# Norm matmuls in another PSUM bank, squares in pairs, and square sums carried over three groups, in a fused attention and channel-mix kernel

## The chip, the cores and the metric

The kernel runs on one core of a Trainium2 chip. The metric is the device time of one execution in microseconds (us). Most executions of a kernel agree within 0.3%; those with a mean granted TensorE clock of 0.988 to 0.997 in place of 0.998 to 1.000 are mostly 0.3 to 4 us longer than the fastest, and a few at 0.998 to 1.000 are longer too, by up to 1 us. I give the lowest time beside the median where that matters.

## The reference

Two stages, with B = 4, N = 6208 and 256 channels, all in fp32:

```python
qn = q / (np.linalg.norm(q, axis=1, keepdims=True) + 1e-06)   # norms over the 6208 rows
kn = k / (np.linalg.norm(k, axis=1, keepdims=True) + 1e-06)
s = kn.transpose(0, 2, 1) @ qn / tau                          # 256 x 256 per batch
a = softmax(s);  x = v @ a
xk = mu_k * x + (1 - mu_k) * x_prev;  xr = mu_r * x + (1 - mu_r) * x_prev
kk = np.maximum(xk @ w_k, 0) ** 2                             # 1024 hidden
out = sigmoid(xr @ w_r) * (kk @ w_v)
```

## The kernel before

After a head that treats the covariance of batch 0, a main loop goes through 48 blocks of 512 rows and one of leftovers. A block has eight steps j. Beside each block's channel mix, the loop builds the covariance and the column norms of the next batch from row groups of 512 (12 full ones per batch and one of 64 rows). Matmuls write into tiles in PSUM. A `tag` names a place there, which with one buffer holds one tile at a time: the next tile of that tag waits until the one before has been copied out. The parts that matter, cut:

```python
def up(i, fh):                                     # hidden slice fh of block i
    kT_ps = ps.tile([P, M], F32, name="kT_ps", tag="kT", bufs=3)
    # ... two matmuls of w_k with xk into kT_ps ...
    kr = p2.tile([P, M], BF16, name="kr", tag="kr", bufs=4)
    nc.scalar.activation(kr[:, :m], kT_ps[:, :m], AF.Relu, scale=RH)

def square(i, fh):
    nc.vector.tensor_tensor(st[i, "kk"][:, fh, :m], kr[:, :m], kr[:, :m], op=OP.mult)

# gate_mm: g_ps lies in the single PSUM bank "g"; x_half: xT_ps lies in the single bank "xT"
# unit(b, g, s): covariance matmuls of a quarter group, then ACT squares it into G["sq", s // 2]

def take_sum():                                    # two adds on DVE for each group
    if w == 1:
        nc.vector.tensor_tensor(G["sq", 0], G["sq", 0], G["sq", 1], op=OP.add)      # 128 x 1024 fp32
        return
    if w == 2:
        nc.vector.tensor_tensor(t1, G["sq", 0][:, 0], G["sq", 0][:, 1], op=OP.add)  # to bf16

def take_norm():                                   # one set of four one-column matmuls for each group
    n_ps = ps.tile([P, 4], F32, name="n_ps", tag="g")
    # ... n_ps[:, 2i+h] = t1 slice (as weights) @ ones ...
    nc.scalar.copy(ssq[b][:, :, g], n_ps)

# in the loop, step j of block i (cut):
up(i + 1, j)
if j == 0: square(i, 7)
if j > 0:  square(i + 1, j - 1)
# ... gate_mm in steps 0, 1, 4, 5; down (the second product, reads kk); x_half in steps 0 and 2 ...
# ... mix_delta in step 4, mix(n, "xk", 0) in step 5, mix(n, "xk", 1) in step 6 ...
# softmax pieces; norms in steps 3 and 7; sums in steps 2, 3, 6, 7
```

## Time and profile before

| | before |
|---|---|
| time, median of 3 runs | 517.29 us (517.14 to 517.46) |
| profiled span | 515.3 us |
| TensorE / VectorE / ScalarE busy | 96% / 88% / 85% |
| matmuls for norms in the loop | 156 |

TensorE is PE in the profile (PEld for its weight loads), VectorE DVE, ScalarE ACT, GpSimd POOL. The profile's own busy share hides how little TensorE loses, so the measure used from here on is this: a weight load starts with the matmul ahead of it, so the starts of loads give the pace of the matmuls (medians 216, 109, 56 and 25 ns for 512, 256, 128 and 1 columns). What the gaps have beyond the pace is **stall**. In the text below it is netted: a late load is often followed by a gap that is shorter than the pace, and both are counted.

The next fence is the timeline of before around one of the longest stalls: start in us, length in us, engine, line, what it does, and in brackets how long the engine had been idle and what released it.

```profile
389.06 0.42 DVE L348 TENSOR_TENSOR kk<-kr 128x512 bf16<-128x512 bf16 x1
389.40 0.75 DVE L324 SCALAR_TENSOR_TENSOR xk<-delta,mu_k_t,X 128x512 bf16<-128x512 bf16 x1
390.06 0.76 DVE L348 TENSOR_TENSOR kk<-kr 128x512 bf16<-128x512 bf16 x2
390.20 0.38 PE L339 MATMUL kT_ps<-xk,w_k_sb 128*128 128x512 bf16 x1 [0.60 <-DVE xk L324]
```

The matmul of the next block's first slice waits for the second half of xk, which VectorE starts (389.40) only after a square (389.06). The chain of waits that ended last is of no use here: it holds 2.5 us near the end only.

### The profile page before, as it was taken

How to read it: one execution, taken by the hardware profiler on the slowest of the kernel's cores; microseconds unless marked ns; L12 is line 12 of the kernel's file. 1: busy time of each engine (PE TensorE's matmuls, PEld its weight loads, DVE VectorE, ACT ScalarE, POOL GpSimd, SP SyncE). 2: the span in 40 equal slices, each digit the busy share in tenths (PEclk: the TensorE clock that was granted, in tenths of full speed). 3: DMA queues.
4: the chain of work that ended last, by engine and by line, in shares of the span. 5: the costliest groups of instructions: out<-in, count | busy, mean ns of one | idle time of the engine just before them, and what ended most of it. 6: DMA issues, size and time to landing. Idle time of an engine off the chain costs nothing. (4 is left out here: it accounts for less than half of the span.)

```text
span 515.3 us, 10233 instructions
## 1 busy us (share of the span) xinstructions
PE 492.3 (96%) x3723; PEld 340.5 (66%) x3786; DVE 451.3 (88%) x899; ACT 435.7 (85%) x832; POOL 104.5 (20%) x145
## 2 busy tenths in 40 slices
PE   4699999999999999999999999999999999999996
PEld 2474676767667677677666767667666666666675
DVE  3468899999999999999999999999989888888884
ACT  5778999999989898899999899899787877777773
POOL 0047523332431231221251132100031000000000
PEclk9999999999999999999999999999999999999999
DMA  8999999999999999599699999962298673332113
GB/s 313 396 321 188 181 201 207 194 201 186 186 186 207 164 170 174 115 173 155 109 185 216 167 178 165 142 129 71 62 170 141 122 126 95 94 88 76 58 67 102
DMA packets 143202, 83.51 MB, mean 162 GB/s; under 512 B 51184, under 2 KB 139824, under 8 KB 143152
## 3 DMA queue, kind: packets, MB, share of 16 engines
q0 software_dynamic: 65808, 33.01, 50.1%
q1 hardware_dynamic: 77184, 49.72, 39.5%
q8 instruction: 29, 0.48, 0.4%
q14 instruction: 21, 0.17, 0.1%
q10 hardware_dynamic: 160, 0.13, 0.1%
HBM read 78.71 MB, written 25.43 MB: 202 GB/s over the span
## 5 line engine op out<-in xcount | busy, mean ns | idle before, releaser
L342 ACT ACTIVATE kr<-kT_ps 128x512 bf16<-128x512 f32 (+1 forms) x392 | 232.5, 595 | 37.0 <-PE kT_ps L339 29.8
L387 PE MATMUL v_ps<-w_v_sb,kk 128*128 128x256 bf16 x1536 | 230.4, 273 | 0.5
L339 PE MATMUL kT_ps<-xk,w_k_sb 128*128 128x512 bf16 (+1 forms) x725 | 218.9, 377 | 3.0 <-DVE xk L324 1.3
L348 DVE TENSOR_TENSOR kk<-kr 128x512 bf16<-128x512 bf16 (+1 forms) x392 | 161.7, 417 | 35.1 <-ACT kr L342 31.4
L387 PEld LDWEIGHTS <-kk 128*128 128x128 bf16 x1536 | 150.2, 98 | 57.6
L430 ACT ACTIVATE sq<-qk 128x512 f32<-128x512 bf16 (+1 forms) x147 | 93.2, 634 | 0.0
L339 PEld LDWEIGHTS <-w_k_sb 128*128 128x128 bf16 x784 | 74.8, 98 | 22.0 <-issue 1.0
L358 PE MATMUL g_ps<-w_r_sb,xr 128*128 128x256 bf16 x388 | 73.9, 272 | 2.5 <-ACT ssq L467 1.3
L260 ACT CAST X<-xT_ps 128x512 bf16<-128x512 f32 x94 | 55.5, 590 | 20.0 <-PE xT_ps L258 19.3
L324 DVE SCALAR_TENSOR_TENSOR xr<-delta,mu_r_t,X 128x512 bf16<-128x512 bf16 x96 | 71.5, 745 | 0.0
L358 PEld LDWEIGHTS <-xr 128*128 128x128 bf16 x388 | 37.8, 98 | 49.0 <-issue 5.9
L324 DVE SCALAR_TENSOR_TENSOR xk<-delta,mu_k_t,X 128x512 bf16<-128x512 bf16 x94 | 70.1, 745 | 0.0
L400 DVE SCALAR_TENSOR_TENSOR res<-res,v_ps 128x512 f32<-128x512 f32 x96 | 65.3, 680 | 0.0
L416 POOL DMA_DIRECT2D qk<-in_q_dram x39 | 28.6, 734 | 164.8 <-ACT sq L430 136.7
L393 ACT ACTIVATE res<-g_ps 128x512 f32<-128x512 f32 x97 | 57.8, 596 | 0.4 <-PE g_ps L358 0.4
L258 PE MATMUL xT_ps<-vT,a_sb 128*128 128x512 bf16 x188 | 55.9, 379 | 0.2 <-ACT X L285 0.2
L426 PE MATMUL s_ps<-qk 128*128 128x256 bf16 (+1 forms) x294 | 56.1, 272 | 0.0
L227 POOL DMA_DIRECT2D v_bf<-in_v_dram x48 | 37.3, 781 | 52.4 <-DMA vT<-v_bf 47.4
L448 DVE TENSOR_TENSOR sq<-sq 128x1024 f32<-128x1024 f32 x36 | 43.9, 1219 | 1.0 <-ACT sq L430 1.0
L426 PEld LDWEIGHTS <-qk 128*128 128x128 bf16 (+1 forms) x294 | 26.6, 97 | 12.1 <-issue 1.3
L313 DVE TENSOR_TENSOR delta<-X 128x1024 bf16<-128x1024 bf16 x48 | 32.9, 686 | 0.1
L416 POOL DMA_DIRECT2D qk<-in_k_dram x39 | 28.9, 741 | 6.8 <-DMA qk<-in_q_dram 2.1
(73 smaller groups left out, 235.1 us busy)
## 6 DMA issues: line engine op xcount, KB each, us to landing
out_dram<-res SPq DMA_DIRECT2D x48, 512.0 KB, 3.3
v_bf<-in_v_dram POOLq DMA_DIRECT2D x48, 256.0 KB, 8.1
qk<-in_q_dram POOLq DMA_DIRECT2D x36, 256.0 KB, 8.5
qk<-in_k_dram POOLq DMA_DIRECT2D x36, 256.0 KB, 9.5
f<-in_q_dram SPq DMA_DIRECT2D x12, 512.0 KB, 8.3
f<-in_k_dram SPq DMA_DIRECT2D x11, 512.0 KB, 9.1
vT<-v_bf SPq DMA_TRANSPOSE x44, 6.7
w_k_sb<-in_moe_w_k_dram POOLq DMA_DIRECT2D x1, 512.0 KB, 6.3
```

Of the source, the lines that this page charges most:

```text
L258: nc.tensor.matmul(xT_ps, a_sb[:, b, ih, dh * P:(dh + 1) * P], vT[:, :, ih, :], start=ih == 0, stop=ih == 1)
L324: nc.vector.scalar_tensor_tensor(o[:, dh], st[i, "d"][:, dh], mu[:, dh:dh + 1], X[:, dh, c:c + M], op0=OP.mult, op1=OP.add)
L339: nc.tensor.matmul(kT_ps[:, :m], w_k_sb[:, dh, fh * P:(fh + 1) * P], xk[:, dh, :m], start=dh == 0, stop=dh == 1)
L342: nc.scalar.activation(kr[:, :m], kT_ps[:, :m], AF.Relu, scale=RH)
L348: nc.vector.tensor_tensor(st[i, "kk"][:, fh, :m], kr[:, :m], kr[:, :m], op=OP.mult)
L358: nc.tensor.matmul(g_ps[:, s % 2], xr[:, dh, s * P:(s + 1) * P], w_r_sb[:, dh, :], start=s % 2 == 0 and dh == 0, stop=dh == 1, skip_group_ ...
L387: nc.tensor.matmul(v_ps[:, s % 2], kk[:, fh, s * P:(s + 1) * P], w_v_sb[:, fh, :], start=s % 2 == 0 and fh == 0, stop=fh == 7, skip_group_ ...
L393: nc.scalar.activation(st[i, "res"][:, 2 * u:2 * u + 2], st.pop((i, "g", u)), AF.Tanh, scale=0.5)
L400: nc.vector.scalar_tensor_tensor(r, r, 1.0, st.pop((i, "v", u)), op0=OP.add, op1=OP.mult)
L416: nc.gpsimd.dma_start(qk[:rows, :n, i], src_rows(t, b, g))
L426: nc.tensor.matmul(cov[b][:, ih, :], qk[:rows, s, 1, ih * P:(ih + 1) * P], qk[:rows, s, 0, :], start=g == GORD[0] and s == 0 and ih == 0, ...
L430: nc.scalar.activation(G["sq", s // 2][:rows, s % 2], qk[:rows, s], AF.Square)
```

## The change

Intent: take norm matmuls off TensorE (one set for three groups in batches 2 and 3), pay for the added fp32 adds by squaring two slices in one operation, and take the norms out of the gate's bank. Norms also run at least two steps after their sum. The core of the diff (cut: bookkeeping of columns, and the flag `bank_x`, which is set when another piece takes the place of x in that step; `T` counts steps):

```diff
-        kr = p2.tile([P, M], BF16, name="kr", tag="kr", bufs=4)
-        nc.scalar.activation(kr[:, :m], kT_ps[:, :m], AF.Relu, scale=RH)
+        if fh % 2 == 0:
+            st[i, "kr", fh // 2] = p2.tile([P, 2, M], BF16, name="kr", tag="kr", bufs=3)
+        nc.scalar.activation(st[i, "kr", fh // 2][:, fh % 2, :m], kT_ps[:, :m], AF.Relu, scale=RH)
...
-        nc.vector.tensor_tensor(st[i, "kk"][:, fh, :m], kr[:, :m], kr[:, :m], op=OP.mult)
+        if fh % 2 == 0:
+            return
+        nc.vector.tensor_tensor(st[i, "kk"][:, fh - 1:fh + 1, :m], kr[:, :, :m], kr[:, :, :m], op=OP.mult)
...
+                m = (GORD.index(g) - 1) % MERGE if b > 1 else 0      # MERGE = 3
+                if m == 0:
+                    sums.append((b, g, 1))                           # acc = sq0 + sq1
+                else:
+                    sums.append((b, g, 3))                           # acc += sq0
+                    sums.append((b, g, 4))                           # acc += sq1
+                if b == 1 or m == MERGE - 1:
+                    sums.append((b, g, 2))                           # t1 = the halves of acc added
...
-        norms.append((b, g, t1))
+        norms.append((b, g, t1, T + 2))
-        n_ps = ps.tile([P, 4], F32, name="n_ps", tag="g")
+        n_ps = ps.tile([P, 4], F32, name="n_ps", tag="xT")
-            nc.scalar.copy(hold["bc"], broadcast(hold["dq"], "g"))
+            nc.scalar.copy(hold["bc"], broadcast(hold["dq"], "xT"))
...
-            if j > 0 and 0 <= i + 1 < NBLK:
+            if j > 0 and j != 6 and 0 <= i + 1 < NBLK:
                 square(i + 1, j - 1)
...                                                                  # after mix(n, "xk", 1):
+            if j == 6 and 0 <= i + 1 < NBLK:
+                square(i + 1, j - 1)
...
-            elif j in (3, 7) or j in (2, 6) and len(norms) > 1:
+            if j in (4, 6) and not bank_x or j in (3, 5) and len(norms) > 1:
                 take_norm()
```

More of the change, by code (lines that the diff above doesn't have):

```diff
@@ L340, in up @@
                              start=dh == 0, stop=dh == 1)
-        kr = p2.tile([P, M], BF16, name="kr", tag="kr", bufs=4)
-        nc.scalar.activation(kr[:, :m], kT_ps[:, :m], AF.Relu, scale=RH)
-        st[i, "kr", fh] = kr
+        if fh % 2 == 0:
+            st[i, "kr", fh // 2] = p2.tile([P, 2, M], BF16, name="kr", tag="kr", bufs=3)
+        nc.scalar.activation(st[i, "kr", fh // 2][:, fh % 2, :m], kT_ps[:, :m], AF.Relu, scale=RH)
     def square(i, fh):
         m = size(i)
-        kr = st.pop((i, "kr", fh))
-        nc.vector.tensor_tensor(st[i, "kk"][:, fh, :m], kr[:, :m], kr[:, :m], op=OP.mult)
+        if fh % 2 == 0:
+            return
+        kr = st.pop((i, "kr", fh // 2))
+        nc.vector.tensor_tensor(st[i, "kk"][:, fh - 1:fh + 1, :m], kr[:, :, :m], kr[:, :, :m], op=OP.mult)
     def gate_mm(i, s):
@@ L422, in unit @@
             ssq[b] = pn.tile([P, 4, NB + 1], F32, name="ssq")
+            ncol[b] = 0
         G = groups[b, g]
@@ L432, in unit @@
             if n == S:
-                sums.append((b, g, 1))
-                sums.append((b, g, 2))
+                m = (GORD.index(g) - 1) % MERGE if b > 1 else 0
[6 more added lines that the diff above has]
+                    sums.append((b, g, 2))
             else:
@@ L439 @@
     norms = []
+    acc = {}
+    MERGE = 3
     def take_sum():
@@ L447, in take_sum @@
         if w == 1:
-            nc.vector.tensor_tensor(G["sq", 0], G["sq", 0], G["sq", 1], op=OP.add)
+            acc[b] = pq.tile([P, 2, 2, C], F32, name="acc", tag="acc", bufs=2)
+            nc.vector.tensor_tensor(acc[b], G["sq", 0], G["sq", 1], op=OP.add)
+            return
+        if w > 2:
+            nc.vector.tensor_tensor(acc[b], acc[b], G["sq", w - 3], op=OP.add)
             return
@@ L451, in take_sum @@
         if w == 2:
-            nc.vector.tensor_tensor(t1, G["sq", 0][:, 0], G["sq", 0][:, 1], op=OP.add)
+            nc.vector.tensor_tensor(t1, acc[b][:, 0], acc[b][:, 1], op=OP.add)
         else:
             nc.vector.tensor_copy(t1[:rows], G["sq", 0][:rows, 0])
-        norms.append((b, g, t1))
+        norms.append((b, g, t1, T + 2))
     def take_norm():
-        if not norms:
+        if not norms or norms[0][3] > T:
             return
-        b, g, t1 = norms.pop(0)
+        b, g, t1, _ = norms.pop(0)
         rows, n = rows_of(g)
-        n_ps = ps.tile([P, 4], F32, name="n_ps", tag="g")
+        n_ps = ps.tile([P, 4], F32, name="n_ps", tag="xT")
         for i in range(2):
@@ L466, in take_norm @@
                                  start=i == 0 and h == 0, stop=True, skip_group_check=True)
-        nc.scalar.copy(ssq[b][:, :, g], n_ps)
+        nc.scalar.copy(ssq[b][:, :, ncol[b]], n_ps)
+        ncol[b] += 1
         if g == GORD[-1]:
@@ L471 @@
     ssq = {}
+    ncol = {}
     s_sb = {}
@@ L482, in a @@
         def a():
-            hold["n"] = root(ssq[b], 4)
+            hold["n"] = root(ssq[b][:, :, :ncol[b]], 4)
         def a2():
@@ L634 @@
                 v_load(i + 7)
-            bank_g = False
-            if chain and (chain[0] is None or chain[0].__name__ != "bcast" or j in (3, 7)):
+            bank_x = i >= 0 and i % NB == 6 and j == 4
+            if chain and (chain[0] is None or chain[0].__name__ != "bcast" or j in (4, 6)):
                 f = chain.pop(0)
@@ L639 @@
                     f()
-                    bank_g = f.__name__ == "bcast"
-            if bank_g:
-                pass
-            elif j in (3, 7) or j in (2, 6) and len(norms) > 1:
+                    bank_x = f.__name__ == "bcast"
+            if j in (4, 6) and not bank_x or j in (3, 5) and len(norms) > 1:
                 take_norm()
```

## The prediction

> **What bounds the kernel now.** I read the page first, engine totals and then the 40 slices, and after that the groups by shape, the waits, and the timeline around single waits of TensorE.
>
> ```profile
> span 515.3 us, 10233 instructions
> ...
> PE 492.3 (96%) x3723; PEld 340.5 (66%) x3786; DVE 451.3 (88%) x899; ACT 435.7 (85%) x832; POOL 104.5 (20%) x145
> ...
> PE   4699999999999999999999999999999999999996
> PEld 2474676767667677677666767667666666666675
> DVE  3468899999999999999999999999989888888884
> ACT  5778999999989898899999899899787877777773
> ```
>
> TensorE (PE) is full from the fourth slice on; VectorE (DVE) and ScalarE (ACT) are nearly full, but behind it. Busy time cannot say how full PE is, so I took the start times of all weight loads (a load starts with the matmul ahead of it, and no load is missing from the trace). From one to the next the median is 109 ns for a matmul of 256 columns, 216 ns for 512, and 25 ns for the one-column norm matmuls. What goes beyond those medians is stall: 22.8 us in the whole span, 14.1 of them in the head before 48 us, which the change does not touch. So in the 467 us of the main loop PE stands still for 8.8 us. No change on DVE or ACT alone can win more than that; the rest must come from fewer matmuls.
>
> The waits of PE, and the groups concerned:
>
> ```profile
> PE g_ps L358 <- ACT ssq L467: 1.3, 4, 0.5
> PE kT_ps L339 <- DVE xk L324: 1.3, 3, 0.6
> PE n_ps L465 <- DVE t L452: 0.5, 1, 0.5
> ```
>
> ```profile
> L348 DVE TENSOR_TENSOR kk<-kr 128x512 bf16<-128x512 bf16 x384 | 159.3, 420 | 32.7 <-ACT kr L342 29.1
> ...
> L448 DVE TENSOR_TENSOR sq<-sq 128x1024 f32<-128x1024 f32 x36 | 43.9, 1219 | 1.0 <-ACT sq L430 1.0
> ...
> L313 DVE TENSOR_TENSOR delta<-X 128x1024 bf16<-128x1024 bf16 x48 | 32.9, 686 | 0.1
> ...
> L452 DVE TENSOR_TENSOR t<-sq 128x512 bf16<-128x512 f32 x36 | 24.6, 684 | 0.0
> ...
> L465 PE MATMUL n_ps<-ones_b,t 128*128 128x1 bf16 x144 | 8.7, 164 | 0.6 <-DVE t L452 0.5
> ```
>
> Two stretches of the timeline, start and length in us. In the first, four norm matmuls are over 0.10 us after they began, though their records last 0.24. In the second, the gate matmuls (g_ps) wait until ACT has copied the norms out of the bank that both use; ACT is late because the softmax's two exponentials came first.
>
> ```profile
> 253.72 0.24 PE L465 MATMUL n_ps<-ones_b,t 128*128 128x1 bf16 x4
> 253.82 0.38 PE L426 MATMUL s_ps<-qk 128*128 128x256 bf16 x2
> ```
>
> ```profile
> 269.41 0.50 ACT L202 ACTIVATE e_sb<-t_sb,nrm_o 128x256 f32<-128x256 f32 x1
> ...
> 270.38 0.16 ACT L467 COPY ssq<-n_ps 128x4 f32<-128x4 f32 x1
> ...
> 270.59 0.38 PE L358 MATMUL g_ps<-w_r_sb,xr 128*128 128x256 bf16 x2 [0.47 <-ACT ssq L467]
> ```
>
> **What the Trainium skill says.** "TensorE: Matmul & The Clock Gate", section "Wait — 56ns, not 53.3ns?", gives N/2.4 + about 2.5 ns from start to start, and about 25 ns as the floor for small N. The trace agrees: 109 and 216 ns, and 25 for one column. "Perfetto Trace Analysis", section "Tensor Engine Instruction (MATMUL, LD_WEIGHTS)", says that a matmul's end is estimated; hence 164 ns records that follow each other after 25, and hence I count starts. "VectorE: DVE Perf Modes", section "The TRN2 errata — SBUF-src ops pay a fixed extra latency per instruction", says a large tile pays a fixed cost once; here 512 bf16 elements more (420 to 686 ns) cost 266 ns, so about 154 of the 420 are fixed. "PSUM — Partial Sum Buffer", section "PSUM bank collisions raise a hardware error", says to guard by bank, not by address: that is the wait for the norms' copy above.
>
> **The change part by part.**
>
> *Fewer norm matmuls.* Before, each of 13 groups in three batches has four: 156. After, batch 1 keeps 13 sets, and batches 2 and 3 have one for the leftover rows and one for each three of 12 groups, so five: 23 sets, 92 matmuls. 64 go, at 25.6 ns: 1.6 us off PE, all on the path. By their busy time (164 ns each) one would expect 10 us; that is the trap. 16 copies of 169 ns leave ACT, 2.7 us, beside the path.
>
> *Sums carried in fp32.* Three groups cost DVE 3 x (1219 + 684) = 5.7 us before, 5 x 1219 + 684 = 6.8 after. Eight times in all: 8.6 us more on DVE.
>
> *Squares in pairs.* 196 operations on 1024 elements in place of 392 on 512. By the records a pair saves 2 x 420 - 686 = 154 ns, 30 us in all. But DVE records overlap their successors by 83 ns (median) where they follow at once: the pace is 337 and 603 ns, so a pair saves about 70 ns, some 14 us, where DVE is backed up, and the full 30 only on paper. A block has 4 pairs: 0.28 us saved, against 0.36 us that the sums add on average in batches 2 and 3. So DVE's load there (229 us busy of 240) stays about where it is; batch 1 and the last 130 us get relief.
>
> *Order and bank.* The fifth and sixth squares now come after the second half of xk. In the trace that half ends only 0.17 us before its matmul in the last stage, 0.40 in most of batches 2 and 3, and is late twice. Ahead of it now stands no square that waits for ACT. The norms and the broadcast go to the bank of x, where x itself is made in steps 0 and 2 of 8; at the end of step 4 the copy of x has been done for 0.7 to 2.0 us, and the next x is due two steps later. Norms now run at least two steps after their sums are queued, so their DVE sum is long done.
>
> What this takes of the 8.8 us of stall in the loop, by position:
> - Gate behind a norm or broadcast copy, nine places: 2.7 us. Goes.
> - Norm matmul waiting for its DVE sum, five places: 2.0 us. Goes.
> - kT waiting for xk, near 370 and 389 us: 1.5 us. Goes.
> - First block at 48 to 51 us: 1.1. Stays.
> - Covariance bank at each change of batch: 1.0. Stays.
> - Tail: 0.4. The last square is a pair of 256 columns and takes 420 in place of 289 ns: 0.13 worse.
>
> Removable 6.2 us. A stall that goes lets PE run up to the next limit, with ACT 93% busy in batch 1, so I take three quarters: 4.7 us. Sum: 1.6 + 4.7 - 0.1 = 6.2 us, and 517.3 - 6.2 = 511.1 us.
>
> **The rivals.**
>
> *DVE becomes the bound in batches 2 and 3.* For: the sums add 8.6 us there, and some blocks get three sums in a row, 2.9 us at pace, where an average block had 1.7. Such a block asks 9.7 us of DVE, as much as PE takes for it. Against: what PE needs soonest (xk) now stands ahead of the squares, and the eighth square has 1.97 us of slack in most of these blocks. If this wins, each of some eight full blocks costs 0.3 to 0.5 us and the time is about 514.
>
> *The pair makes the second matrix product late.* A pair starts only when its second half is there and takes 0.27 us longer. Matmuls of the next block need it 1.97 us after the single square's end now, 1.67 in the last stage, with a least value of 0.6 early, where DVE is backed up. Against all of that 0.27 is small. If it did bite in all 48 blocks it would cost 13 us, and the kernel would be slower, near 524.
>
> *The new bank is as busy as the old.* One norm, in block 6 of batch 1, falls in step 3, right behind x, and four pieces share the bank with the leftover rows. A few waits of 0.3 us: 512.
>
> *Everything removable goes.* 517.3 - 1.6 - 6.2 = 509.5 us. Nothing lies below that save the 1.1 us of the first block, so over 2% (507.0) is nearly out of reach.
>
> **Range and chances.** Full gain is 509.5, half the stalls 512.6, only the matmuls 515.7. I put 8 in 10 on 508.9 to 514.4 with 511.1 in the middle. Faster by over 2%: 0.03, as it needs a gain that PE's own list does not have. Slower by over 2%: 0.02, only by late pairs. Within 2%: 0.95.
>
> **What would show it.** In the profile after: 92 norm matmuls and 23 copies; kk at about 686 ns, 52 fp32 adds at about 1219; the waits of PE for ssq, for t and for xk gone; stall in the loop near 4 us by the starts of weight loads; DVE busy 425 to 445 us; a span near 509. Wrong would be: waits of xT_ps or n_ps on a copy of x or of norms; v_ps waiting for kk; kT_ps for xk inside batches 2 and 3 (rival one); or stalls gone and the same length back as waits for ACT's kr.

## The result

The changed kernel takes 511.51 us (median of 4, 511.43 to 512.42) against 517.38 us for before (median of 4, 517.14 to 520.59). The ratio is 0.9876, with a 95% interval of 0.9836 to 0.9916; within 2%. Ratios are the mean time of one kernel's fast runs over that of the other's of the same rounds, so not quite the ratio of these medians.

From the page of after, the span, the engines and the 40 slices:

```profile
span 509.7 us, 9775 instructions
...
PE 493.9 (97%) x3722; PEld 339.3 (67%) x3722; DVE 444.7 (87%) x703; ACT 431.8 (85%) x816; POOL 106.2 (21%) x145
...
PE   5799999999999999999999999999999999999996
...
DVE  3467798999999999999999999999998787878884
```

The span is 5.6 us shorter. PE's busy time went up by 1.6 us although it has 64 matmuls less: before, part of the records were missing (63 of its matmuls; its 3786 loads were all there). VectorE lost 196 operations and only 6.6 us of busy time.

The waits of PE after 46 us in after (total us, number, longest):

```profile
PE kT_ps L339 <- DVE xk L324: 0.5, 2, 0.3
PE xT_ps L258 <- ACT vT L251: 0.2, 1, 0.2
PE v_ps L375 <- DVE res L402: 0.2, 1, 0.2
```

The waits for ssq and for t are gone, that for xk is not. The groups by shape of after that answer to those shown of before:

```profile
L350 DVE TENSOR_TENSOR kk<-kr 128x1024 bf16<-128x1024 bf16 x192 | 130.9, 685 | 31.6 <-ACT kr L343 31.0
...
L464 DVE TENSOR_TENSOR acc<-acc,sq 128x1024 f32<-128x1024 f32 x32 | 39.0, 1220 | 1.0
...
L461 DVE TENSOR_TENSOR acc<-sq 128x1024 f32<-128x1024 f32 x20 | 24.4, 1218 | 2.4 <-ACT sq L433 2.4
...
L468 DVE TENSOR_TENSOR t<-acc 128x512 bf16<-128x512 f32 x20 | 13.8, 688 | 0.4
...
L481 PE MATMUL n_ps<-ones_b,t 128*128 128x1 bf16 x80 | 4.8, 164 | 0.0
```

A pair takes 685 ns, 52 fp32 adds about 1219 ns each, and 92 norm matmuls are left (12 of them on 64 rows, in a group not shown). VectorE between 130 and 370 us, where batches 2 and 3 lie, from the stretches view (each number the engine's busy us, in brackets its instructions; PE, PEld, DVE, ACT, POOL in this order), first of before, then of after:

```profile
130.00:370.00 240.00, 237.37 (x1765) 166.18 (x1796) 229.27 (x444) 217.95 (x435) 52.88 (x71) 1.00 0.96 158
...
130.00:370.00 240.00, 239.51 (x1752) 166.29 (x1750) 231.66 (x351) 215.45 (x422) 56.52 (x73) 1.00 1.04 157
```

VectorE has 229.3 us before and 231.7 us after. The pairs pay for the adds there, and no more.

The stall in the loop, sorted by what stands at its place in the trace (us, netted):

| what TensorE stands for | before | after |
|---|---|---|
| gate behind a norm or broadcast copy in its bank | 2.7 | 0 |
| norm matmul behind its DVE sum | 1.0 | 0 |
| kT behind xk | 1.5 | 1.0 |
| step to the 64-row leftovers and back | 1.2 | 1.2 |
| first block and a half | 0.6 | 0.7 |
| tail | 0.4 | 0.5 |
| sum | 7.4 | 3.4 |

4.0 us of stall and 64 x 25.3 ns = 1.6 us of matmuls are 5.6 us: all that the span lost. The head's stall is the same in the two profiles (12.4 and 12.5 us, netted).

### The profile page after: what moved, and what is told of

Read it like the earlier page. It is cut to its first block, busy times and chain, and to the rows that moved or that the text cites.

```text
span 509.7 us, 9775 instructions
## 1 busy us (share of the span) xinstructions
PE 493.9 (97%) x3722; PEld 339.3 (67%) x3722; DVE 444.7 (87%) x703; ACT 431.8 (85%) x816; POOL 106.2 (21%) x145
## 5 line engine op out<-in xcount | busy, mean ns | idle before, releaser
L339 PE MATMUL kT_ps<-xk,w_k_sb 128*128 128x512 bf16 (+1 forms) x784 | 231.5, 377 | 0.5 <-DVE xk L324 0.5
L350 DVE TENSOR_TENSOR kk<-kr 128x1024 bf16<-128x1024 bf16 (+1 forms) x196 | 132.6, 680 | 34.4 <-ACT kr L343 33.7
L324 DVE SCALAR_TENSOR_TENSOR xk<-delta,mu_k_t,X 128x512 bf16<-128x512 bf16 x94 | 66.1, 744 | 0.0
L464 DVE TENSOR_TENSOR acc<-acc,sq 128x1024 f32<-128x1024 f32 x32 | 39.0, 1220 | 1.0
L429 PEld LDWEIGHTS <-qk 128*128 128x128 bf16 (+1 forms) x294 | 27.4, 98 | 12.3 <-issue 1.3
## 6 DMA issues: line engine op xcount, KB each, us to landing
out_dram<-res SPq DMA_DIRECT2D x48, 512.0 KB, 3.8
f<-in_q_dram SPq DMA_DIRECT2D x12, 512.0 KB, 8.2
f<-in_k_dram SPq DMA_DIRECT2D x11, 512.0 KB, 9.1
w_k_sb<-in_moe_w_k_dram POOLq DMA_DIRECT2D x1, 512.0 KB, 8.1
```

The costliest lines, as they stand in the source:

```text
L324: nc.vector.scalar_tensor_tensor(o[:, dh], st[i, "d"][:, dh], mu[:, dh:dh + 1], X[:, dh, c:c + M], op0=OP.mult, op1=OP.add)
L339: nc.tensor.matmul(kT_ps[:, :m], w_k_sb[:, dh, fh * P:(fh + 1) * P], xk[:, dh, :m], start=dh == 0, stop=dh == 1)
L350: nc.vector.tensor_tensor(st[i, "kk"][:, fh - 1:fh + 1, :m], kr[:, :, :m], kr[:, :, :m], op=OP.mult)
L429: nc.tensor.matmul(cov[b][:, ih, :], qk[:rows, s, 1, ih * P:(ih + 1) * P], qk[:rows, s, 0, :], start=g == GORD[0] and s == 0 and ih == 0, ...
```

## The experiments

Twelve kernels ran, all with correct results. The edits are against before for the first three and against the changed kernel for the rest. In each table row the last column is the before kernel's 517.1 us, plus the difference of stall to before's 7.4 us, plus 25.3 ns for each norm matmul above or below 156.

| kernel | median (lowest), us | ratio to before, 95% interval | norm matmuls | stall in the loop, us | time from stall and matmuls, us |
|---|---|---|---|---|---|
| changed kernel | 511.51 (511.43) | 0.9836 to 0.9916 | 92 | 3.4 | 511.5 |
| bank alone | 515.00 (514.79) | 0.9947 to 0.9973 | 156 | 5.2 | 514.9 |
| merge alone | 522.13 (520.86) | 1.0081 to 1.0119 | 92 | 13.1 | 521.2 |
| pairs alone | 516.86 (516.55) | 0.9990 to 1.0036 | 156 | 7.0 | 516.7 |
| no merge | 513.43 (512.37) | 0.9914 to 0.9938 | 156 | 2.9 | 512.5 |
| square not moved | 515.73 (515.66) | 0.9934 to 0.9983 | 92 | 7.5 | 515.5 |
| norms four times | 517.83 (517.62) | 0.9991 to 1.0033 | 368 | 2.8 | 517.8 |
| full rows | 511.87 (511.52) | 0.9871 to 0.9909 | 92 | 3.5 | 511.6 |
| sums spread | 511.01 (510.70) | 0.9855 to 0.9893 | 92 | 3.0 | 511.0 |
| full rows, sums spread | 511.30 (510.91) | 0.9870 to 0.9907 | 92 | 3.0 | 511.1 |
| scale late | 513.27 (512.63) | 0.9889 to 0.9932 | 92 | 4.7 | 512.8 |
| full rows, spread, late | 513.39 (513.01) | 0.9892 to 0.9951 | 92 | 5.2 | 513.2 |
| full rows, spread, scale on ScalarE | 512.50 (512.12) | 0.9874 to 0.9919 | 92 | 4.0 | 512.0 |

That sum, worked out before rounding, meets the medians of all of them within 1.0 us, and the lowest times within 0.4. It is a reading of one profile for each kernel, not a model that foretells anything; but it says that TensorE's stalls and its matmuls are the whole of the time outside the head. What is left over lies in the head: its netted stall, up to 48 us, is 12.4 us in the profile of before and 12.3 to 14.4 in the others, though no edit touches it. With that difference added, the sum meets the time of each profiled execution itself within 0.25 us. Differences of a us or less between medians can so be the head's alone.

### The three parts, each alone

**Bank alone.** Only the take_norm, broadcast and step conditions of the diff, on before: the new bank and the two steps of delay together.

> The kernel before with one part of the change: norm matmuls and broadcast in the bank of x, in steps 4 and 6 (3 and 5 when two are queued), two steps after their sums. Theory (stalls of TensorE decide): the gate's waits for copies out of its bank, 2.7 us, and the real waits of a norm for its DVE sum, 1.1 us, go, and nothing comes back: 3.8 us less, about 513.5 us, no g_ps wait for ssq. Rival (the new bank is as busy as the old one): waits of xT_ps or n_ps for copies appear and the gain is under 1.5 us, 516 us or more.

Measured: 515.0 us, 2.1 less than before. Neither forecast met it. The waits of the gate and of the norms are gone from PE's list, as the theory said, and no wait for a copy came in their place, so the rival's cause is out too. But in that list (bank alone, after 46 us) this stands first:

```profile
PE kT_ps L339 <- DVE xk L324: 2.3, 6, 0.6
```

By the starts of loads, kT behind xk has grown from 1.5 to 2.9 us, at 145, 155, 264, 274 and 371 us. TensorE, freed of 3.7 us, ran into VectorE, and 1.5 us came back.

**Merge alone.** Only the carried sums and their columns, on before.

> The kernel before with the carried fp32 sums alone: 92 norm matmuls in place of 156, squares single, norms still in the gate's bank. Theory: 64 matmuls at 25.6 ns are worth 1.6 us, and the two long waits of the gate for a norm copy behind the exponentials (0.64 us each) may go, as fewer norms are there; against that VectorE gets 8.6 us more in batches 2 and 3, where it is nearly full and xk has only 0.06 to 0.7 us of slack, so kT waits for xk in the full blocks: between 514.5 and 517.5 us, with the xk wait grown to over 1.5 us. Rival (a norm matmul costs what its record lasts, 164 ns): 10 us less, about 507.

Measured: 522.1 us, 5.1 slower (4.0 by the lowest times), beyond what either side foresaw. The direction of the theory held (VectorE is full there, xk comes late), its size did not. PE's waits of this kernel after 46 us:

```profile
PE kT_ps L339 <- DVE xk L324: 3.7, 8, 0.6
PE n_ps L479 <- DVE t L466: 2.8, 5, 0.7
PE vT_ps L247 <- DMA v_bf<-in_v_dram: 2.1, 1, 2.1
```

About 5.4 us of stall stand behind xk and 4.0 behind t; the wait for a DMA ends at 45.9 us, in the head of this one execution, and is not in the 13.1. The two long waits of the gate behind the exponentials went, as expected (gate waits 1.4 us in place of 2.7). I had left out the waits for t: in this kernel a norm may come in the very next slot after its sum, which stands in a queue of long adds.

**Pairs alone.** Only kr, square and the moved call, on before.

> The kernel before with the squares in pairs and the third pair moved behind xk, alone. Theory: only the waits of kT for xk go, 1.5 us, and 0.13 come back in the tail, so 516.0 us, though VectorE loses 15 to 30 us of work: the gate's and the norms' waits stay. Rival (VectorE is the bound): 8 us or more less. Rival (late pairs): slower than before, with v_ps waiting for kk.

Measured: 516.9 us, and the interval of the ratio holds 1. Taking 12 us of busy time off VectorE (407.4 from 419.4 us, between 52 and 508 us) moves the time by 0.2 to 0.4 us. The xk stalls went from 1.5 to 0.7 us, not to nothing; a norm's wait for t at 114 us grew by 0.2 and the tail by 0.13. VectorE is not the bound of before, and late pairs are not seen.

The three alone come to -2.1, +5.1 and -0.2 us, a sum of +2.8 (by the lowest times -2.1, +4.0 and -0.3, a sum of +1.6). Together they are -5.9 (-5.7). Each part lives off the others.

### What the merge is worth in company

**No merge.** The changed kernel without the carried sums.

> The changed kernel without the carried sums: bank and pairs, 156 norm matmuls. Theory: 1.6 us more of matmuls, but VectorE is lighter in batches 2 and 3, so the three waits of kT for xk that the changed kernel has (1.0 us together) shrink or go: 0.6 us slower than the changed kernel, about 512.1. Rival (the carried sums cost nothing on the path): 1.6 us slower, 513.1, with the same xk waits.

Measured: 513.4 us with clocks down to 0.995 in its runs, lowest 512.4; the changed kernel 511.5, lowest 511.4, in other rounds. So the merge gains about 1 to 2 us where pairs and bank are there; the intervals of the two ratios just touch. The median is nearer to the rival's 513.1, but the profiled execution has 0.8 us more stall in the head than before has, and the waits are the theory's. The stalls behind xk are 0.4 us here against 1.0 in the changed kernel, as the theory said: 1.6 us of matmuls less 0.6 us of stall make 1.0, a little more than forecast. Alone, the same edit cost 5.1 us.

**Norms four times.** Its edit wraps the set in a loop:

```diff
+        for _ in range(4):
             for i in range(2):
                 for h in range(2):
                     nc.tensor.matmul(n_ps[:, 2 * i + h:2 * i + h + 1], ...)
```

> The changed kernel with every set of norm matmuls issued four times over (the last pass gives the right values): 276 more of them, nothing else. Theory (a norm matmul costs TensorE 25 ns): 7.0 us more than the changed kernel's 511.5, about 518.5. Rival (it costs what its record lasts, 164 ns): 45 us more, 556.

Measured: 517.8 us. With the 0.6 us of stall that this kernel has less, 276 more matmuls cost 6.3 + 0.6 = 6.9 us, 25 ns each. The groups by shape of this kernel show records of 163 ns all the same:

```profile
L482 PE MATMUL n_ps<-ones_b,t 128*128 128x1 bf16 x320 | 10.8, 163 | 0.0
```

That settles the price of a norm matmul.

### The moved square

**Square not moved.** The changed kernel with the call at its old place:

```diff
-            if j > 0 and j != 6 and 0 <= i + 1 < NBLK:
+            if j > 0 and 0 <= i + 1 < NBLK:
                 square(i + 1, j - 1)
...
-            if j == 6 and 0 <= i + 1 < NBLK:
-                square(i + 1, j - 1)
```

> The changed kernel with the third pair of squares back in its old place, ahead of the second half of xk. Theory: there the pair takes 0.6 us of VectorE's pace, and has to wait for ScalarE first, so xk's second half, whose slack in the changed kernel is 0.57 us in the last stage and 0.1 to 1.3 us in batches 2 and 3, is late in many blocks: kT waits for xk grow from 1.0 us to 4 us or more, and the time to 514.5 or more. Rival (the move is cosmetic): 511.5.

Measured: 515.7 us, 4.2 slower than the changed kernel, with 5.1 us of stall behind xk at 22 places: ten up to 370 us, of 0.06 to 0.9 us, and twelve in the last stage, each 0.09. PE's wait in this kernel's list, over all the span, which counts only the long ones:

```profile
PE kT_ps L339 <- DVE xk L324: 2.3, 5, 0.7
```

Among the other parts, this one call order is worth more (4.2 us) than the bank gains alone on before (2.1).

### What is left, and the 64-row leftovers

**Full rows.** The leftover groups filled up with zeros:

```diff
         groups[b, g] = {"qk": qk}
+        if rows < P:
+            nc.gpsimd.memset(qk[rows:, 0], 0.0)
...
     def unit(b, g, s):
-        rows, n = rows_of(g)
+        rows, n = P, rows_of(g)[1]      # and rows = P in take_sum and take_norm
```

> The changed kernel with the leftover group of 64 rows filled up with zeros to 128 for its covariance and norm matmuls (one memset on GpSimd for each of three batches). Theory: what I had put down in the prediction to a late DVE sum and to the covariance bank is TensorE going from 128 rows to 64 and back, about 0.2 us each time; six such places, 1.2 us, go: 510.3 us. Rival (they are waits for data or banks): nothing changes, 511.5.

The timeline of after at one such place, PE and its loads:

```profile
127.49 0.21 PEld L258 LDWEIGHTS <-a_sb 128*128 128x128 bf16 x2
127.60 0.59 PE L258 MATMUL xT_ps<-vT,a_sb 128*128 128x512 bf16 x2
128.12 0.11 PEld L429 LDWEIGHTS <-qk 64*128 64x128 bf16 x2 [0.42 <-issue]
128.13 0.39 PE L429 MATMUL s_ps<-qk 64*128 64x256 bf16 x2
128.44 0.11 PEld L339 LDWEIGHTS <-w_k_sb 128*128 128x128 bf16 x2 [0.21 <-issue]
```

And the same place with full rows:

```profile
127.34 0.59 PE L258 MATMUL xT_ps<-vT,a_sb 128*128 128x512 bf16 x2
127.55 0.31 PEld L431 LDWEIGHTS <-qk 128*128 128x128 bf16 x2
127.77 0.38 PE L431 MATMUL s_ps<-qk 128*128 128x256 bf16 x2
```

With 64 rows, the first load starts after the matmuls ahead, not beside them (128.12 against their start at 127.60 with two of 0.216 us to go); the first load of 128 rows after it does the same. The way there and back costs 0.21 us for a covariance pair and 0.19 for a norm set. With full rows the loads run ahead again, and all six such stalls, 1.2 us, are gone from the trace. So the attribution is shown. The time, though, is 511.9 us: nothing gained. The stalls behind xk went from 1.0 to 2.0 us, at the three places that they had before (153, 269 and 366 us). What TensorE was spared, it waited for VectorE; the other 0.3 us came up in the first blocks. Both sides of the forecast were half right.

**Sums spread.** In the changed kernel two or three adds stand together ahead of xk:

```diff
+        if n == S and s == 1 and b > 1 and (GORD.index(g) - 1) % MERGE:
+            sums.append((b, g, 3))
         if s == n - 1:
...
-                    sums.append((b, g, 3))
                     sums.append((b, g, 4))
```

> The changed kernel with the first carried add of a group queued after its second quarter in place of its fourth, so that two or three adds no longer stand together in steps 1 to 3 ahead of xk. Theory: the three waits of kT for xk, 1.0 us together, come from adds piled up in one block on VectorE; they shrink to under 0.3 us: 510.6 us. Rival (they come from the softmax pieces, or from TensorE being faster): they stay, 511.5.

Measured: 511.0 us, half of the forecast gain. The stalls behind xk went from 1.0 to 0.27 us, as the theory said: those at 154 and 270 us are gone, so the piled-up adds made them, and that at 366 us is halved; but matmuls of v_ps now wait for kk at 156 and 272 us, 0.14 us each, which the changed kernel does not do. Its median is the lowest of the study, 0.5 us under the changed kernel's, but in other rounds: the mean ratios to before are 0.9874 and 0.9876, so that the two differ is not shown.

**Full rows and sums spread together.**

> Full rows and spread adds together on the changed kernel. Theory: the two are separate stalls of the same engine, so they add: 509.4 us. Rival (what one frees is taken by the next wait): 510.3 or more.

Measured: 511.3 us; the rival was right. The stalls are 3.0 us, no fewer than with spread adds alone, though the 1.2 us of the row steps are gone: behind xk there are 0.3 us each at 153, 270 and 366 us, and the waits of v_ps for kk, at four places from 146 to 273 us, come to 0.65 us.

**Scale late.** I took the last softmax piece for the cause of what is left and held it back:

```diff
-            if chain and (chain[0] is None or chain[0].__name__ != "bcast" or j in (4, 6)):
+            if chain and (chain[0] is None or chain[0].__name__ != "bcast" or j in (4, 6)) and \
+                    (chain[0] is None or chain[0].__name__ != "f" or j == 7):
```

> The changed kernel with the last softmax piece (two reciprocals and two scalings on VectorE) held back from step 0 of blocks 9, 21 and 33 to step 7, nothing else. Theory: in blocks 9 and 21 that piece and two carried adds stand ahead of xk on VectorE, which runs without a gap there, so the xk waits at 154 and 270 us (0.52 us together) go, the one at 366 us stays: 511.0 us. Rival (the adds alone are at fault): no change, 511.5.

> Full rows, spread adds and the late softmax piece together. Full rows alone gave nothing because VectorE's work ahead of xk in blocks 9 and 21 took what they freed. Theory: with that work moved the freed time is kept, stalls in the loop go from 3.4 to about 1.8 us, and the time to 509.9 us, below every kernel so far. Rival (VectorE is full in batches 2 and 3 whatever the order): no less than 510.7, with v_ps waiting for kk in place of kT for xk.

Measured: 513.3 and 513.4 us, 1.8 and 1.9 us slower than the changed kernel. Both theories failed; the rival of the second (no less than 510.7) was right in number only. The xk wait at 154 us did go and that at 270 us shrank, so that piece stands in the same queue as the adds; but the x matmuls of the next batch read what that piece writes, one step later. From PE's list in the second kernel, after 46 us:

```profile
PE xT_ps L258 <- DVE a_sb L207: 1.9, 2, 1.0
```

I had set the deadline from the order of the program and not from VectorE's backlog.

**Full rows, spread, scale on ScalarE.**

```diff
         def f():
-            for ih in range(2):
-                soft_scale(b, ih, e_sb, sm)
+            nc.vector.reciprocal(sm, sm)
+        def f2():
+            for ih in range(2):
+                nc.scalar.activation(a_sb[:, b, ih, :], e_sb[:, ih], AF.Copy, scale=sm[:, ih:ih + 1])
-        return [a, None, a2, b1, None, bcast, None, c, e, f]
+        return [a, None, a2, b1, None, bcast, None, c, e, f, None, f2]
```

> Full rows and spread adds on the changed kernel, and the softmax's last scalings moved from VectorE to ScalarE two steps later, with one reciprocal for both halves. Holding that piece back on VectorE only moved the wait to the x matmuls. Theory: in the blocks where the softmax falls VectorE's work itself is the limit, not its order; 0.9 us less of it at 146 and 263 us takes away the xk waits there (0.3 us each in full rows and spread adds together) and half of the waits for kk just behind: stalls in the loop from 3.0 to about 2.2 us, 510.4 us, the fastest kernel here. Rival (ScalarE is the limit there): kr comes later, DVE waits more for it, and the time is 511.3 or more.

Measured: 512.5 us; the rival was right. The timeline of this kernel:

```profile
150.87 0.94 ACT L530 ACTIVATE a_sb<-e_sb,sm 128x256 bf16<-128x256 f32 x2
...
152.33 0.69 DVE L350 TENSOR_TENSOR kk<-kr 128x1024 bf16<-128x1024 bf16 x1 [0.93 <-ACT kr L343]
```

ScalarE takes 0.94 us for the scalings and is late with kr, so VectorE idles 0.93 us and xk is late again (0.47 us at 154 and at 271 us). In the blocks where a softmax falls, ScalarE has no more room than VectorE.

## Why the prediction was right, point by point

The time (511.1 foretold, 511.5 measured) and the class were right, and the balance of the trace closes. The terms:

- *64 norm matmuls at 25.6 ns, 1.6 us.* Right. Norms four times confirms 25 ns for each.
- *Gate behind copies, nine places, 2.7 us, goes.* Right: 2.7 to 0, and nothing came into the bank of x in its place. Bank alone shows it without the other parts. Two remarks on the reading: ahead of the copy at 270.38 us ScalarE had not only the two exponentials but also a kr (269.90, 0.58 us); and n_ps and g_ps are tiles of one tag with one buffer, so they would wait for each other whatever the rule for banks.
- *Norm matmul waiting for its DVE sum, five places, 2.0 us, goes.* Mis-sized, and partly a wrong cause. Three of the five places were steps to 64 rows and back, 0.19 us each; full rows shows it. The true term was 1.0 us netted, and that went.
- *Covariance bank at each change of batch, 1.0, stays.* It stayed, but at 0.4 us and for another cause: full rows took it away without touching the bank. I also counted only the long gaps and not the short ones behind them, which is why the loop's stall was 8.8 us in the prediction and 7.4 when netted.
- *kT waiting for xk, 1.5 us, goes.* Failed: 1.0 us is left, of it 0.5 in batches 2 and 3 where before had none. That is the first rival, VectorE full in those batches, at a sixth of the size feared. Sums spread shows that the piled-up adds make it, together with the softmax piece in the same queue (scale late).
- *Three quarters of the removable 6.2 us.* 4.0 us came off in place of 4.7. That a flat three quarters came so near was in part luck: it covered the two faults above, which I did not know of, and the reason that I gave for it, ScalarE in batch 1, was wrong. Batch 1 kept all that it won. What came back was at VectorE in batches 2 and 3 and behind them.
- *VectorE's load there stays about where it is.* Right: 229.3 and 231.7 us of 240. The second half of that, which the prediction did not state, is that neither the merge nor the bank is worth its own without the pairs and the moved square.
- *Late pairs.* Not seen in the changed kernel to speak of. With spread adds, waits of 0.14 us behind kk appear twice.
- *The tail, 0.13 us worse.* Right: 0.41 to 0.54 us.

Open: whether a version with less work on VectorE in the softmax blocks reaches the 1.2 us of the row steps. Moving that work, late or to ScalarE, did not. Not run either: the moved square without the pairs. Pairs alone and no merge hold both, and square not moved takes away only the move (4.2 of the 5.9 us), so how much of the gain needs the pairs themselves, and not just the order, is not shown.

## What to carry to other kernels

Where one engine is full, list its stalls by place before anything else, by starts and netted, and read off the list what a change can win; here stalls and matmuls matched the medians of thirteen kernels within 1.0 us, and with the head counted each profiled execution within 0.25. A part that is worth little or is harmful alone (pairs, merge) can be what makes another pay, so test parts in company too. When a stall goes and the time does not, look which wait grew at the next deadline of the second-fullest engine, and mind the order of what it still has to do: one call moved behind xk was worth 4.2 us here.

## What the Trainium skill lacked or had wrong

- "TensorE: Matmul & The Clock Gate", section "The mechanism" in Part 3, says under "What overlaps and what doesn't" that a weight load overlaps with matmuls in flight only when its row group differs (the text just above it, in the same section, also allows a load into a background weight buffer). In the trace of before 3648 of the 3786 loads are loads on all 128 rows that start about 2 ns after a matmul on all 128 rows, and it is the load on 64 rows, and the first on 128 after it, that wait. No page gives the cost of that step, 0.19 to 0.21 us there and back; full rows shows that it comes and goes with the 64 rows, not what causes it.
- The same page, section "Back-to-back issue gap", gives 131 ns for each matmul of 512 columns and 81 ns for 128 in a stream of loads and matmuls. Here such streams run at 216 and 56 ns, which is the formula that the page calls isolated.
